# A planner's costs, from estimates to measured durations, and a margin behind the landing of raw weights

## The chip, the cores and the metric

The kernel runs on one core of a Trainium2 chip. Time is device microseconds (us) of one execution, lower is better. Five engines work side by side, each through its own list of instructions in order: TensorE (PE for its matmuls, PEld for its weight loads), VectorE (DVE), ScalarE (ACT), GpSimd (POOL) and SyncE (SP), which issues nearly all transfers.

## What is computed

Attention over 8 batches and 8 heads (576 positions, head size 64) with a window of 128 positions and a bias that falls with distance, and on its output (4608 tokens of 512 numbers) a gated feed-forward layer of width 1536. All inputs of the second part come as 64-bit floats.

```python
scores = scale * np.matmul(q, k.transpose(0, 1, 3, 2))
scores = np.where(mask, scores + bias[None], -1000000000.0)   # 0 <= rel < 128
scores = scores - np.max(scores, axis=-1, keepdims=True)
attn = np.exp(scores)
attn = attn / (np.sum(attn, axis=-1, keepdims=True) + 1e-09)
x = np.matmul(attn, v)             # transposed to (4608, 512)
gate = 1.0 / (1.0 + np.exp(-(x @ w_gate)))
val = x @ w_val
out = gate * val @ w_out
```

## The kernel before

**Attention.** A unit is one batch and one pair of heads; there are 32, of 9 blocks of 128 rows each, so 288 blocks. `scores` sends a run of eight blocks (four for the first units) through TensorE (line 440) into four PSUM banks, in a mode that splits the array into quarters of 64 rows by 64 columns. VectorE puts the window's far side in place (line 457) and adds the bias and takes the row maximum in one operation (line 465); ScalarE takes the exponential and the row sum (line 469). Three blocks make a triple, of which there are 96: `probabilities` divides them by their sums (a scaling for each block, on ScalarE, line 547, or on VectorE, line 548), TensorE transposes the three (line 554), a copy takes them out of PSUM and GpSimd cuts them into two masked halves (line 565). The values matmuls follow, for the first 11 units in `values` (line 592), for the others in `split_values` (line 511): two phases in the same quartered mode, usually one on either side of a scores run.

**First pass.** For the first 3072 tokens and the first 4 of 12 slices of the hidden width, gate and value products are made while attention still runs (line 640; 576 matmuls in all, in groups of three, called chunks here). Their weights are decoded from 64-bit words by `decode`: a transfer of 512 KB into one of two raw buffers (`wraw`), a scaling on ScalarE (line 331), a shift and two merges on VectorE (lines 332 and 335); then a high part and a remainder are formed (lines 195, 196, 204), since a product is made of three matmuls on split numbers.

**Second pass and output.** When attention has ended, its buffers are given back, the attention output is read again from device memory (`later_xr`), seven combinations of it are made (`xc`, lines 737, 195, 196, 204), and the other slices (and these four for the remaining tokens) follow as seven products in place of eight (line 774, 2016 matmuls, with the sums and gates of lines 781, 785 and 789). Their weights (`w2s`, seven slots) are decoded, combined and split on VectorE and ScalarE while these products run. The last stage does the same for the output weights (line 904, 1260 matmuls).

**What sets the order.** Nothing in the code orders the engines by hand. Every operation is put down with `g.add`: engine, cost in us, what it reads and writes, a wish (`want`), a `slack` that is added to the time at which its readers or it may go, and sometimes other engines that could do it. `Graph.order` then plays this list: again and again it takes the operation that can start and end soonest by these costs, chooses the engine, and notes a start; the program is written out in the order of the starts. First-pass and second-pass products have the lowest wish, so they go wherever the plan believes TensorE free. The costs decide the order only; what the chip takes is its own matter.

In `order`, an operation becomes ready like this, and `d.slack` is the place at which the change's new margin enters:

```python
same = o.eng == "PE" and d.eng == "PE"
d.ready = max(d.ready, o.start + (o.cost if same else o.lat + d.slack))
```

Of the kernel before, what the change touches and what calls it, by code (L numbers as in the profile page):

```python
# [20 lines left out]
DM, DFF = 512, 1536  # L21
# [34 lines left out]
SLACK = 0.1  # L56
W0, WSTEP = 20.0, 2.0
SWITCH = 0.36
WARM = 30.0
YIELD = {"DVE": 0.1, "POOL": 0.0}  # L60
NRAW = 2
# [3 lines left out]
def as32(ap):  # L65
    return ap.bitcast(F32)
# [102 lines left out]
def act_cost(n, psum=False):  # L169
    return (0.05 if psum else 0.1) + n * 0.00084  # L170
# [3 lines left out]
def attention_gated_ffn(ctx: ExitStack, tc: tile.TileContext, qd, kd, vd, wg, wv, wo, out):  # L174
    nc = tc.nc
    ctx.enter_context(tc.manual_schedule())
    g = Graph()
# [29 lines left out]
    mm = [ps_m.tile([P, NB], F32, name=f"mm{i}") for i in range(8)]  # L207
# [114 lines left out]
    def decode(src, fc, bits, kb, want, release=0.0):  # L322
        s = raws[0] % NRAW
        raws[0] += 1
        kr = ("wraw", s)
# [3 lines left out]
        raw = lambda: T(moe, f"wraw{s}", [P, DM, 2], I32)  # L329
        move(lambda: raw().rearrange("p f t -> p (f t)"), lambda: src[fc].bitcast(I32), [], [kr], want, 512, True, release)  # L330
        g.add("ACT", act_cost(DM), lambda: nc.scalar.mul(as32(bits()), as32(raw()[:, :, 1]), 2.0 ** -112), [kr], [kb], want)
        g.add("DVE", dve_cost(DM), lambda: nc.vector.tensor_scalar(
# [78 lines left out]
    def scores(blks, pend=None):  # L411
# [31 lines left out]
        for (u, i), (r, a) in zip(blks, spot):  # L443
            used.setdefault(bank_of(r, a), []).append((u, i, a % 2))
        cost = sum(max(0.216 if i == 0 else 0.33 for (u, i), (r, b) in zip(blks, spot) if b == a) for a in {a for r, a in spot})
        reads = [("qr", u.l, i) for u, i in blks] + [("kr", u.l, j) for u, i in blks for j in (i - 1, i) if j >= 0]
# [40 lines left out]
    def split_values(u, want, reads, writes, release):  # L487
# [15 lines left out]
        def phase(n, reads, writes, release):  # L503
# [3 lines left out]
            def matmuls():  # L507
                for e, r, h, j, a, b, first, last in runs:
# [4 lines left out]

            g.add("PE", 0.85, matmuls, need + [("vr", u.l)] + ([("turn", u.s)] if n else []) + reads, both + writes, want, slack=0.0 if n else SLACK,
                  release=release, mode=1)
# [20 lines left out]
    def probabilities(u, i0):  # L536
# [8 lines left out]
        for e in range(n):  # L545
            args = lambda e=e: (pb()[:, e], pb()[:, e], st()[:, 6 + e:7 + e])
            g.add("ACT", 0.3, lambda args=args: nc.scalar.mul(*args()), [(kst, 6)], [(kpb, e)], want,  # L547
                  ways=[("DVE", 0.16, True, lambda args=args: nc.vector.tensor_scalar_mul(*args()))])

        z = work()  # L550
# [4 lines left out]

        g.add("PE", 0.11 * n + 0.1, transpose, [(kpb, e) for e in range(n)], [("mm", z)], want, slack=slack)
        copy(lambda: both(), lambda: mm[z][:, 0:n * P].rearrange("p (a q) -> p a q", a=n), n * P, [("mm", z)], [kb], want, psum=True)
# [528 lines left out]
```

## Time and profile before

| | us |
|---|---|
| median of 3 runs | 981.16 |
| lowest and highest of them | 978.7 and 981.19 |
| the profiled execution's own time | 983.17 |
| its span, first to last instruction | 981.5 |
| TensorE busy, matmuls | 964.4 (98%) |
| TensorE busy, weight loads | 833.6 (85%) |
| VectorE busy | 771.6 (79%) |
| ScalarE busy | 531.7 (54%) |
| GpSimd busy | 126.5 (13%) |

The ends of matmuls in the profile are modelled and overlap, so 98% is no measure of how well TensorE is fed; it shows where TensorE stood idle, not how fast it went elsewhere. The shares are means over stages that differ: attention with the first pass until about 312 us, the second pass until about 709 us, the output stage until the end. Scores and values matmuls stand twice in the trace for each one in the program's listing.

### The profile page before, as it was taken

Reading aid. Unit: us, or ns where it says so; the run is one execution under the profiler, and the core shown is the slowest. Engines: PE = TensorE matmul, PEld = TensorE weight load, DVE = VectorE, ACT = ScalarE, POOL = GpSimd, SP = SyncE. Lnnn points to the kernel's source line nnn. Section 1 sums busy time; section 2 is a strip of 40 time slices with the busy share of each in tenths; the row PEclk is TensorE's granted clock in tenths of the full one; section 3 lists DMA queues with packets and bytes.
Section 4 is the critical chain, followed back from the end, with each engine's and each line's share of the span. In section 5 each row is a group of like instructions: output and inputs, shape, how many; then the busy total and the mean of one; then the engine's idle time right before and its main releaser. Section 6 shows DMA issues by size and latency. Waiting matters only on the chain.

```text
span 981.5 us, 18510 instructions
## 1 busy us (share of the span) xinstructions
PE 964.4 (98%) x6588; PEld 833.6 (85%) x6588; DVE 771.6 (79%) x1933; ACT 531.7 (54%) x1413; POOL 126.5 (13%) x213
## 2 busy tenths in 40 slices
PE   8899999999999999999999999999999999999998
PEld 7666788888878999999988888888878888889998
DVE  8998879977767999937984885793578977877783
ACT  8998878878874556434543443352344433333341
POOL 2333445333333000000000100000000000000000
PEclk9999999999999999999999999999999999999999
DMA  8868877775715535334374274469775435262601
GB/s 312 272 207 298 302 229 271 252 251 167 254 59 174 185 106 188 121 117 151 150 273 172 119 278 150 162 242 344 250 272 189 163 99 190 64 193 81 194 17 65
DMA packets 82078, 186.03 MB, mean 190 GB/s; under 512 B 7745, under 2 KB 36801, under 8 KB 81985
## 3 DMA queue, kind: packets, MB, share of 16 engines
q1 hardware_dynamic: 81840, 184.71, 54.7%
q8 instruction: 52, 0.85, 0.4%
q14 instruction: 42, 0.34, 0.1%
q10 hardware_dynamic: 144, 0.13, 0.0%
HBM read 122.95 MB, written 61.87 MB: 188 GB/s over the span
## 4 chain that ended last, share of the span: by engine, by line
PE 80%; DVE 8%; ACT 6%; DMA 4%; issue 1%; POOL 0%; POOLq 0%; ACTq 0%; DVEq 0%; SPq 0%
PE mm L774 40%; PE mm L904 25%; PE mm L640 7%; PE mm L440 3%; PE mm L511 2%; ACT pb L469 2%; PE mm L554 1%; DVE mm L457 1%; DVE first L204 1%; DVE pb L465 1%; DMA hid<-later_hs 1%; DVE wbits L335 1%; PE mm L592 1%; DMA rows_h<-hid 1%; DMA wraw<-in_moe_w_gate_dram 1%
## 5 line engine op out<-in xcount | busy, mean ns | idle before, releaser
L774 PE MATMUL mm<-xc,w2s 128*128 128x384 f32 (+1 forms) x2016 | 404.4, 362 | 0.2 <-DVE xc L204 0.2
L774 PEld LDWEIGHTS mm<-xc,w2s 128*128 128x128 f32 x2016 | 363.8, 188 | 40.7 <-DVE xc L204 0.6
L904 PE MATMUL mm<-duo,wo 128*128 128x512 f32 (+1 forms) x1260 | 259.2, 367 | 1.6 <-DVE duo L204 1.6
L904 PEld LDWEIGHTS mm<-duo,wo 128*128 128x128 f32 x1260 | 229.2, 188 | 31.6 <-DVE duo L204 2.0
L640 PE MATMUL mm<-first,first 128*128 128x512 f32 x576 | 155.6, 407 | 1.4 <-ACT sg L651 0.9
L640 PEld LDWEIGHTS mm<-first,first 128*128 128x128 f32 x576 | 101.6, 189 | 23.7 <-ACT sg L651 1.9
L785 ACT ACTIVATE sg<-mm 128x384 f32<-128x384 f32 (+1 forms) x96 | 52.2, 545 | 110.6 <-PE mm L774 71.5
L781 DVE TENSOR_TENSOR mm<-mm,low 128x384 f32<-128x384 f32 (+1 forms) x96 | 60.5, 630 | 64.1 <-PE mm L774 64.0
L195 ACT COPY low<-mm 128x384 f32<-128x384 f32 (+1 forms) x95 | 50.7, 535 | 73.6 <-PE mm L774 70.5
L469 ACT ACTIVATE pb<-pb,st 128x128 f32<-128x128 f32 x216 | 84.8, 401 | 1.6 <-DVE st L465 1.3
L565 POOL TENSOR_SCALAR_AFFINE_SELECT pt<-early_h 128x384 f32<-128x384 f32 x96 | 53.2, 572 | 108.0 <-ACT early_h L195 106.4
L565 POOL TENSOR_SCALAR_AFFINE_SELECT pt<-early_xr 128x384 f32<-128x384 f32 x96 | 52.1, 567 | 54.6 <-ACT early_xr L195 54.5
L457 DVE COPY_PREDICATED mm<-early_h,mm 128x256 f32<-128x256 int32 (+1 forms) x144 | 49.1, 392 | 6.3 <-PE mm L440 6.0
L465 DVE CUSTOM_DVE_ANT_0 pb<-mm,early_h 128x128 f32<-128x128 f32 x216 | 51.2, 282 | 0.0
L511 PEld LDWEIGHTS mm<-pt,vr 64*64 64x64 f32 x924 | 37.2, 132 | 10.5 <-issue 4.3
L547 ACT ACTIVATE pb<-pb,st 128x128 f32<-128x128 f32 x131 | 43.0, 398 | 0.1
L195 ACT COPY early_xr<-mm 128x384 f32<-128x384 f32 (+3 forms) x78 | 33.8, 446 | 16.5 <-PE mm L511 12.5
L469 ACT ACTIVATION_READ_ACCUMULATOR pb<-pb,st 128x1 f32 x216 | 42.7, 198 | 0.0
L542 DVE TENSOR_SCALAR st<-st 128x3 f32<-128x3 f32 x96 | 23.8, 249 | 23.8 <-ACT pb L469 12.4
L511 PE MATMUL mm<-pt,vr 64*64 64x192 f32 (+2 forms) x924 | 41.2, 285 | 0.8 <-ACT turn L520 0.8
L789 DVE SCALAR_TENSOR_TENSOR later_hs<-sg,later_hs 128x384 f32<-128x384 f32 (+1 forms) x48 | 29.9, 622 | 10.4 <-ACT sg L785 10.3
L781 DVE TENSOR_TENSOR later_hs<-mm,later_hs 128x384 f32<-128x384 f32 (+1 forms) x48 | 29.8, 621 | 10.5 <-ACT sg L785 6.8
(138 smaller groups left out, 1229.9 us busy)
## 6 DMA issues: line engine op xcount, KB each, us to landing
hid<-later_hs SPq DMA_DIRECT2D x24, 512.0 KB, 3.4
wo<-stash_o SPq DMA_DIRECT2D x12, 896.0 KB, 7.5
vr<-in_v_dram SPq DMA_DIRECT2D x32, 288.0 KB, 4.8
hid<-later_hs SPq DMA_DIRECT2D x24, 384.0 KB, 2.8
stash_o<-wtmp SPq DMA_DIRECT2D x12, 768.0 KB, 4.0
wraw<-in_moe_w_gate_dram SPq DMA_DIRECT2D x16, 512.0 KB, 5.1
wraw<-in_moe_w_val_dram SPq DMA_DIRECT2D x16, 512.0 KB, 4.5
kr<-in_k_dram SPq DMA_DIRECT2D x11, 576.0 KB, 4.4
```

The source lines that it names most:

```text
L195: g.add("ACT", act_cost(n, psum), lambda: nc.scalar.copy(out(), src()), reads, writes, want, release=release, ways=[("DVE", dve_cost(n, ps ...
L457: g.add("DVE", dve_cost((a1 - a0) * P, psum=True), lambda b=b, a0=a0, a1=a1: nc.vector.copy_predicated(quads(b)[:, a0:a1, 1:3], before[:, ...
L465: g.add("DVE", 0.21, lambda: nc.vector.tensor_tensor_reduce(pb()[:, e], sp[b][:, a, D:D + P], relm[u.p][:, w], op0=ALU.add, op1=ALU.min, s ...
L469: g.add("ACT", 0.39, lambda: nc.scalar.activation(pb()[:, e], pb()[:, e], AF.Exp, bias=st()[:, e:e + 1], scale=-1.0, accum_out=st()[:, 3 + ...
L511: nc.tensor.matmul(mm[WORK[h]][e * D:(e + 1) * D, a - e * S - cuts[h]:b - e * S - cuts[h]], vraw(u)[r * D:r * D + D, c], seen, start=first ...
L547: g.add("ACT", 0.3, lambda args=args: nc.scalar.mul(*args()), [(kst, 6)], [(kpb, e)], want, ways=[("DVE", 0.16, True, lambda args=args: nc ...
L565: nc.gpsimd.affine_select(pt(u)[:, f0:f0 + 2 * n - 1:2, :], both(), [[0, n], step], cmp, 0.0, base=0, channel_multiplier=mult)
L640: nc.tensor.matmul(mm[s][:, 0:wd], w.tile(kind, wi, i)[:, c * P:(c + 1) * P], xpart(x, c)[:, 0:wd], start=(k == 0 and c == 0), stop=(k == ...
L774: nc.tensor.matmul(mm[b][:, 0:N2], w.tile2(i, wp)[:, wk, c * P:(c + 1) * P], combo(k, xp, N2)[:, c], start=(start and c == 0 and j == 0), ...
L781: g.add("DVE", dve_cost(N2, psum=True), lambda: nc.vector.tensor_tensor(o(), bk(b)(), a(), op=ALU.add), [("mm", b), *reads] if okeys else ...
L785: g.add("ACT", act_cost(N2, psum=True), lambda: nc.scalar.activation(sg[h](), bk(b)(), AF.Tanh, scale=0.5), [("mm", b)], [("sg", h)], F)
L904: nc.tensor.matmul(mm[b][:, 0:N2], wo2(2 * q + m, wp)[:, k, j * P:(j + 1) * P], duo(xp)[:, m], start=(k in (0, 3, 1) and q == 0 and m == 0 ...
```

## The change

Six edits of the planner's figures. The scaling of raw weights may start, in the plan, only 4.0 us after the planned landing of its transfer (the margin enters through `slack`). A pair of blocks in a scores run costs 0.29 (0.19 where it is a first block) instead of 0.33 (0.216); one phase of the split values 0.71 instead of 0.85; a scaling of probabilities on VectorE 0.19 instead of 0.16; a triple of transposes 0.095 x 3 = 0.285 instead of 0.11 x 3 + 0.1 = 0.43. No instruction's operands, shapes or buffers are changed; the number of some instructions changes with the engine that the plan chooses for them, and the filler matmuls on `ident` (line 277) with its gaps.

```diff
+LATE = 4.0
@@ decode
-        g.add("ACT", act_cost(DM), lambda: nc.scalar.mul(as32(bits()), as32(raw()[:, :, 1]), 2.0 ** -112), [kr], [kb], want)
+        g.add("ACT", act_cost(DM), lambda: nc.scalar.mul(as32(bits()), as32(raw()[:, :, 1]), 2.0 ** -112), [kr], [kb], want, slack=LATE)
@@ scores
-        cost = sum(max(0.216 if i == 0 else 0.33 for (u, i), (r, b) in zip(blks, spot) if b == a) for a in {a for r, a in spot})
+        cost = sum(max(0.19 if i == 0 else 0.29 for (u, i), (r, b) in zip(blks, spot) if b == a) for a in {a for r, a in spot})
@@ split_values
-            g.add("PE", 0.85, matmuls, need + [("vr", u.l)] + ([("turn", u.s)] if n else []) + reads, both + writes, want, slack=0.0 if n else SLACK,
+            g.add("PE", 0.71, matmuls, need + [("vr", u.l)] + ([("turn", u.s)] if n else []) + reads, both + writes, want, slack=0.0 if n else SLACK,
@@ probabilities
-                  ways=[("DVE", 0.16, True, lambda args=args: nc.vector.tensor_scalar_mul(*args()))])
+                  ways=[("DVE", 0.19, True, lambda args=args: nc.vector.tensor_scalar_mul(*args()))])
-        g.add("PE", 0.11 * n + 0.1, transpose, [(kpb, e) for e in range(n)], [("mm", z)], want, slack=slack)
+        g.add("PE", 0.095 * n, transpose, [(kpb, e) for e in range(n)], [("mm", z)], want, slack=slack)
```

The changed kernel's lines stand one further down than those of before (331 is 332, 774 is 775, and so on), since a constant is added above them.

Nearly every row of the order moves. Three places show how. The first is SyncE's list where attention ends: `xs` is the attention output on its way to device memory, `later_xr` the same data read back for the second pass, `hid` a finished piece of the first pass, `wraw` raw weights. Before:

```order
L200 DMA xs_108<-early_xr 128x576
L200 DMA xs_108<-xt_536 128x576
L200 DMA hid_117<-early_hs_1094 128x512
L200 DMA later_xr<-xs_106 128x4x384
L200 DMA later_xr<-xs_107 128x4x384
L200 DMA hid_132<-early_hs_1217 128x512
L200 DMA wraw_213<-in_moe_w_gate_dram 128x1024
L200 DMA wraw_220<-in_moe_w_val_dram 128x1024
```

and now:

```order
L201 DMA xs_108<-early_xr 128x576
L201 DMA xs_108<-xt_506 128x576
L201 DMA later_xr<-xs_106 128x4x384
L201 DMA later_xr<-xs_107 128x4x384
L201 DMA hid_117<-early_hs_1008 128x512
L201 DMA hid_132<-early_hs_1117 128x512
L201 DMA later_xr<-xs_108 128x4x384
L201 DMA later_xr<-xs_107 128x4x192
L201 DMA later_xr<-xs_108 128x4x192
L201 DMA wraw_221<-in_moe_w_val_dram 128x1024
L201 DMA wraw_215<-in_moe_w_gate_dram 128x1024
```

The first two reads of `later_xr` now follow the last write of `xs` directly, and the raw weights stand behind all five reads. On TensorE, in the same place, the number of first-pass matmuls behind the last values matmul falls from 66 (22 chunks) to 27 (9 chunks), and the second pass opens with combination `xc0` where it opened with `xc3`.

The second is VectorE's list from its last copy of attention's output on (`early_hs` is the first pass's gating, `w2s` a slot of second-pass weights, `low` and `later_xr` as targets are combinations). Before:

```order
L196 COPY xt_536<-mm_78 128x256
L659 SCALAR_TENSOR_TENSOR early_hs_1094<-sg_975,mm_71 128x512
L196 CAST w2s_4228<-wbits_396 128x512
L196 CAST w2s_4228<-tt 128x1280
L659 SCALAR_TENSOR_TENSOR early_hs_1217<-sg_979,mm_72 128x512
L204 TENSOR_TENSOR w2s_4243<-wbits_396,w2s_4228 128x512
L204 TENSOR_TENSOR w2s_4243<-tt,w2s_4228 128x1280
L204 TENSOR_TENSOR w2s_4258<-wbits_390,w2s_4230 128x512
L332 TENSOR_SCALAR wbits_396<-wbits_396 128x512
L332 TENSOR_SCALAR tt<-tt 128x512
```

and now:

```order
L197 COPY xt_506<-mm_78 128x256
L660 SCALAR_TENSOR_TENSOR early_hs_1008<-sg_859,mm_71 128x512
L205 TENSOR_TENSOR w2s_4290<-wbits_438,w2s_4279 128x512
L205 TENSOR_TENSOR w2s_4297<-wbits_418,w2s_4287 128x512
L205 TENSOR_TENSOR w2s_4290<-tt,w2s_4279 128x1280
L660 SCALAR_TENSOR_TENSOR early_hs_1117<-sg_933,mm_72 128x512
L197 CAST xc_4305<-later_xr 128x2x384
L205 TENSOR_TENSOR xc_4305<-later_xr,xc_4305 128x2x384
L205 TENSOR_TENSOR xc_4307<-later_xr,xc_4307 128x2x384
L333 TENSOR_SCALAR wbits_438<-wbits_438 128x512
```

Before, the decoding of a further slot's weights (lines 332 and 335) stands ahead of the first combination; now two combinations come first.

The third is ScalarE's list early in attention, at the third scaling of raw weights. Before, it stands behind 54 exponentials:

```order
L195 COPY early_xr<-mm_78 128x288
L469 ACTIVATE early_h_147,st_366<-early_h_147,st_366 128x128 x2
L469 ACTIVATE early_xr,st_433<-early_xr,st_433 128x128
L195 COPY early_xr<-mm_77 128x288
L469 ACTIVATE early_xr,st_433<-early_xr,st_433 128x128 x2
L331 ACTIVATE wbits_390<-wraw_213 128x512
L195 COPY early_xr<-mm_78 128x384
```

and now behind 63:

```order
L196 COPY early_xr<-mm_78 128x384
L470 ACTIVATE pb_274,st_217<-pb_274,st_217 128x128 x2
L470 ACTIVATE pb_297,st_231<-pb_297,st_231 128x128 x3
L332 ACTIVATE wbits_418<-wraw_215 128x512
L196 COPY xt_506<-mm_77 128x288
L548 ACTIVATE pb_306<-pb_306,st_298 128x128
```

All later scalings of the early stage move back likewise.

## The prediction

> **What bounds the kernel now.** I read the page's busy times, then a table of windows cut at the kernel's stages (span, then busy microseconds and count for PE, PEld, DVE, ACT and POOL, granted clock, DMA share, GB/s), then the chain and the timeline where stages meet.
>
> ```profile
> PE 964.4 (98%) x6588; PEld 833.6 (85%) x6588; DVE 771.6 (79%) x1933; ACT 531.7 (54%) x1413; POOL 126.5 (13%) x213
> ...
> 0.00:42.00 42.00, 36.78 (x423) 28.68 (x424) 36.83 (x215) 36.73 (x150) 12.10 (x27) 0.96 0.84 299
> 42.00:112.00 70.00, 64.92 (x634) 48.10 (x633) 64.88 (x290) 66.45 (x252) 25.94 (x48) 1.00 0.75 257
> 112.00:297.50 185.50, 184.08 (x2194) 151.54 (x2192) 145.69 (x717) 147.06 (x575) 74.09 (x131) 1.00 0.65 217
> 316.00:404.00 88.00, 88.00 (x507) 87.45 (x506) 85.21 (x153) 48.21 (x90) 3.46 (x1) 1.00 0.47 150
> 404.00:709.00 305.00, 305.00 (x1462) 266.97 (x1461) 212.68 (x315) 125.19 (x213) 4.88 (x5) 1.00 0.53 196
> 730.00:981.50 251.50, 247.74 (x1210) 219.83 (x1210) 195.41 (x209) 90.06 (x113) 0.00 (x0) 1.00 0.39 126
> ```
>
> From 112 us on TensorE sets the time: it lacks 1.4 us in 185.5 and nothing from 316 to 709. Before that no engine is alone: from 42 to 112 us it stands idle for 5.1 of 70 us, while VectorE is 93% and ScalarE 95% busy. The number of matmuls is the same in both kernels, so a new order can only fill or open holes. There are two places for that: the stage before 112 us, and the seam at 312 us where attention hands over to the second pass. The turn to the output stage at 709 us is touched by no edit.
>
> The same table for the first pass's matmuls alone (line 640; PE, PEld, clock, DMA, GB/s) and for the transposes (line 554) tells how far the program is at those marks:
>
> ```profile
> 0.00:42.00 42.00, 0.38 (x2) 0.36 (x3) 0.96 0.84 299
> 42.00:112.00 70.00, 26.58 (x96) 16.43 (x94) 1.00 0.75 257
> ...
> 0.00:42.00 42.00, 6.26 (x33) 3.69 (x33) 0.96 0.84 299
> 42.00:112.00 70.00, 14.00 (x74) 8.69 (x75) 1.00 0.75 257
> ```
>
> By 112 us some 36 triples of transposes (107 of them) and 98 first-pass matmuls are out.
>
> **The costs that the planner now uses.** A stretch of the chain from the stage that TensorE fills (start, length, what), then VectorE's scalings in it earlier on:
>
> ```profile
> 263.16 0.85 PE mm L511 x19
> 264.00 1.31 PE mm L440 x27
> 265.32 0.76 PE mm L511 x18
> 266.08 0.89 PE mm L640 x3
> 266.97 0.66 PE mm L554 x6
> 267.63 0.69 PE mm L640 x3
> ...
> 275.15 3.43 PE mm L640 x15
> ...
> 18.54 0.96 DVE pb L548 x5
> ```
>
> A triple of transposes takes 0.66 / 2 = 0.33 us: the plan had 0.43 and gets 0.285. Values, scores, values take 2.92 with one change of array mode in them; the change costs 0.89 - 0.69 = 0.20, so 2.72 bare: the plan had 0.85 + 1.32 + 0.85 = 3.02 and gets 0.71 + 1.16 + 0.71 = 2.58. A scaling on VectorE takes 0.96 / 5 = 0.19, the new figure. So the plan was 0.10 to 0.30 too long on these and is now 0.05 to 0.15 too short: nearer. No instruction becomes shorter by it. What moves is the filler: three matmuls of the first pass (a chunk) take 0.69 to 0.70 us, and the planner puts one wherever it believes TensorE free. Counted over the listed orders: with the 36th triple 32 chunks are out before and 38 after; after the last values matmul 22 stand before and 9 after.
>
> **Edit by edit, early stage.** The six chunks, 6 x 0.70 = 4.2 us, go into the stage with 5.1 us of visible idleness. Their own load elsewhere is small, one gating on VectorE or one tanh on ScalarE per four chunks:
>
> ```profile
> L659 DVE SCALAR_TENSOR_TENSOR early_hs<-sg,mm 128x512 f32<-128x512 f32 x21 | 14.3, 681 | 4.7 <-PE mm L640 4.6
> ```
>
> So six chunks bring about one such operation of 0.7 us. I let them fill holes, -4.2; bounds 0 (every hole lies where a chunk's data isn't there) and -5.1. The later scaling of raw weights acts on ScalarE, which is in order: behind a waiting scaling stand exponentials and the copies out of PSUM, and VectorE's mask and TensorE's transposes wait for those. Line 331's rows up to 115 us (what ended the idle time before it: us, times) show what it waited:
>
> ```profile
> L331 ACT ACTIVATE wbits<-wraw x10: 650/672/707, 19.1 to 114.7; 128x512 f32<-128x512 f32 x10
>   DMA wraw<-in_moe_w_val_dram: 1.7, 1
>   DMA wraw<-in_moe_w_gate_dram: 0.9, 2
> ```
>
> That is 2.6 us. Besides, up to the 36th triple ScalarE's list holds two weight scalings (0.67 each) and three casts of much the same length fewer, about 3 us; VectorE's holds seven scalings of probabilities more (7 x 0.19) and about as much less of the decoding, so its sum stays. With VectorE at 93% I don't believe the whole 5.6: the stage ends between 0 and 4 us sooner, and I take 1.0, near VectorE's side, since that engine gets no lighter. The raw buffers are held up to 4 us longer, which I cost at nothing: the first chunk stands behind the 12th triple instead of the 11th, but at the 19th the new list is ahead, 10 chunks to 6.
>
> **Mode changes.** Counted, 103 become 112; five of the nine lie in the early stage beside idle time, four behind it: 4 x 0.20 = +0.8 (bounds 0 and 1.8).
>
> **The seam.** The timeline before (start, us, engine and line, [idle before]); SPq rows are transfers issued:
>
> ```profile
> 297.49 15.26 PE L640 MATMUL mm<-first,first 128*128 128x512 f32 x66
> 312.58 2.62 PE L774 MATMUL mm<-xc,w2s 128*128 128x384 f32 x14
> 315.44 1.84 PE L774 MATMUL mm<-xc,w2s 128*128 128x384 f32 x9 [0.25 <-DVE xc L204]
> ...
> 298.14 0.32 SPq L200 DMA_DIRECT2D xs<-xt  x1
> 299.89 0.32 SPq L200 DMA_DIRECT2D hid<-early_hs  x1
> 300.39 0.98 SPq L200 DMA_DIRECT2D later_xr<-xs  x2
> ...
> DMA to landing us min/median/max: 3.6/4.4/6.6
> ...
> 308.56 0.95 DVE L737 TENSOR_TENSOR low<-later_xr 128x768 f32<-128x768 f32 x1
> ...
> 358.36 0.56 DVE L196 CAST xc<-later_xr 128x768 fp32r<-128x768 f32 x1
> 359.02 0.96 DVE L204 TENSOR_TENSOR xc<-later_xr,xc 128x768 fp32r<-128x768 f32 x1
> ```
>
> Call V the moment at which the last values matmul ends (297.5). Before, 66 matmuls cover V to 312.6, and the rows `later_xr`, needed for the second pass, are asked for at V + 2.9, behind a write of `hid` that waits for VectorE. After, they stand on SP right behind `xs<-xt`: V + 0.65 + 0.35 = V + 1.0, the second one 0.4 later, and with the longest landing of these reads, 6.6, they are there at V + 8.0. The first combination is then cast (0.66 with its follow-up) and its low part taken (0.95): the first matmuls go at V + 8.7, the third waits until V + 9.6. The cover is now 9 x 0.70 = 6.3 us. So TensorE idles 2.4, then 0.5 for the low part, and some 0.7 while VectorE makes the seven combinations one by one: 3.6 against the 0.25 seen before, net +3.3. Bounds: with the median landing of 4.4 the first matmuls go at V + 6.5, so +1.1; with `hid` writes sharing the transfer engines I allow once more the 2.2 between median and longest, so +5.5.
> [...]
>
> **What is late next.** VectorE prepares the second pass's weights from V on, and must have made the seventh slot when the seventh slice of its first group of tokens starts, then seven new combinations:
>
> ```profile
> 345.05 1.49 DVE L204 TENSOR_TENSOR w2s<-tt,w2s 128x1280 fp32r<-128x1280 f32 x1
> 354.25 0.57 DVE L781 TENSOR_TENSOR mm<-mm,low 128x384 f32<-128x384 f32 x1 [0.57 <-PE mm L774]
> ```
>
> Before, that slot is ready at 346.5 and first used near 356 (six slices of 42 matmuls behind 312.6, at 88.00 / 507 = 0.174 us each; VectorE already waits for TensorE at 354): 10 us of slack. After, with 6 us less cover and the slot's last part ten operations (10 x 0.56) later in VectorE's list, about nothing is left; the new list of TensorE goes round it by starting the second group. I take 0; bounds 0 and +2.
>
> **Sum**, against the profiled span of 981.5 (that execution's time is 983.17; the median of the runs is 981.16, so I carry the difference over to the median): -4.2 - 1.0 + 0.8 + 3.3 + 0 = -1.1. Predicted 980.1 us. V itself moves from 297.5 to about 297.5 + 13 x 0.70 - 5.2 + 0.8 = 302.2.
>
> **The rivals.** (1) Faster: ScalarE alone was the early stage's limit. For it: 95% busy, and the waits of transposes for its copies, below; against it: VectorE's 93%. Then the stage ends 4 us sooner instead of 1.0, and with the median landing the seam costs 1.1: -4.2 - 4.0 + 0.8 + 1.1 = -6.3, 974.9; halfway there, 977.5. Chance 0.28.
> (2) Slower: the cover is gone and the holes stay. The moved chunks then stretch the stage before 112 us by what they take, because holes there come from exponentials and copies that a chunk in front delays too; only the seam's price is left: 0 + 0.8 + 3.3 to 5.5, so 985.3 to 987.5. It decides as soon as fewer than two of the six chunks find a hole. For it: the holes are small, the longest put down to one wait there 0.9 us. Against it: VectorE and ScalarE have 5% or more left. Chance 0.17. The wait both rivals speak of, from 42 to 115 us (us, times, longest):
>
> ```profile
> PE mm L554 <- ACT early_xr L195: 1.7, 2, 0.9
> PEld mm L554 <- ACT early_xr L195: 3.2, 4, 1.4
> ```
>
> (3) The plan's figures change the list but not the time, since TensorE is full from 112 us on and the two places cancel: 981.2, within 1. This runs into my own forecast; both together 0.47.
> (4) The clock. The rows between 34 and 40 us (last columns as above):
>
> ```profile
> 34.00:36.00 2.00, 1.32 (x18) 0.88 (x18) 2.00 (x15) 2.00 (x10) 1.51 (x4) 1.00 0.95 340
> 36.00:38.00 2.00, 2.00 (x20) 1.25 (x20) 2.00 (x14) 1.89 (x10) 0.44 (x1) 0.52 0.58 182
> 38.00:40.00 2.00, 2.00 (x23) 1.96 (x21) 1.73 (x11) 0.47 (x2) 0.00 (x0) 0.63 0.86 276
> ```
>
> After a sparse stretch the granted clock falls to about half for some 3.4 us. If the seam's hole of 2.4 to 3.6 us does the same, half of 3.4 us is lost: +1.7, so 981.8, and with the late landing 984.0. Chance 0.08. [...]
>
> **How the numbers follow.** A measurement of this kernel tells 0.3%, 2.9 us, from no change: its three runs lie 2.5 apart. My forecast and rival (3), 0.47, lie inside, with a tenth of it spilling to either side; (1) is faster; (2) and the late part of (4) are slower. That gives faster 0.31, same 0.45, slower 0.24. The likeliest case alone spans 977.5 to 983. The range reaches from (1)'s far end to near (2)'s: 974.5 to 985.5.
>
> **What would show it.** First-pass matmuls by the 36th triple: 114 by about 111 us, if the holes were filled; if that mark comes at 115 or later, (2) holds. V near 302, `later_xr` asked for about 1 us behind it, a hole of 2 to 4 us before the first matmul of line 775, and full TensorE from some 316 us on. TensorE idle before a slice in the 40 us after that would mean VectorE's weights are late, which I cost at nothing. The last two stages must take what they took, 305 and 251.5 us; if they differ by over 1 us, my sum is wrong whatever its total.

## The result, and the profile after

The changed kernel takes 987.71 us (median, 986.61 to 988.38) against 980.89 for the kernel before on the same chip: a ratio of 1.0073, 95% interval 1.0055 to 1.0091. It is slower; 980.1 was forecast, in a range that ended at 985.5. The profiled execution took 988.38 us, its span 986.7.

The page's busy line and its costliest group, then the same windows as before (span, busy us and count of PE, PEld, DVE, ACT, POOL, granted clock, DMA share, GB/s):

```profile
PE 965.4 (98%) x6604; PEld 838.4 (85%) x6604; DVE 771.7 (78%) x1936; ACT 533.4 (54%) x1405; POOL 123.7 (13%) x218
...
L775 PE MATMUL mm<-xc,w2s 128*128 128x384 f32 (+1 forms) x2016 | 408.7, 364 | 9.9 <-ACT later_hs L196 6.8
...
42.00:112.00 70.00, 67.86 (x661) 53.40 (x661) 64.94 (x285) 66.65 (x250) 25.39 (x48) 0.99 0.82 267
112.00:297.50 185.50, 185.23 (x2181) 153.68 (x2179) 149.31 (x724) 147.83 (x565) 68.44 (x126) 1.00 0.66 216
316.00:404.00 88.00, 87.18 (x502) 86.58 (x501) 83.65 (x148) 43.90 (x85) 4.10 (x4) 1.00 0.49 157
404.00:709.00 305.00, 298.01 (x1414) 259.82 (x1414) 208.23 (x308) 126.16 (x211) 13.69 (x12) 0.99 0.51 189
730.00:981.50 251.50, 251.50 (x1228) 223.01 (x1227) 199.90 (x212) 93.04 (x115) 0.00 (x0) 1.00 0.42 134
```

Attention is better fed than before: TensorE's idle time from 42 to 112 us falls from 5.1 to 2.1 us, from 112 to 297.5 from 1.4 to 0.3. The loss is in a stage that had none: between 404 and 709 us TensorE lacks 7.0 us, 6.8 of them in one wait on `later_hs`. Where that lies is seen when the starts of the same matmul are set side by side (us; counted in the traces; the experiments' columns are read further down):

| mark | before | after | x1 | x2 | x3 | x4 | x5 | x6 | x9 |
|---|---|---|---|---|---|---|---|---|---|
| 36th triple of transposes | 112.0 | -1.5 | -0.7 | +1.3 | -2.4 | +3.4 | -0.8 | -5.5 | -0.6 |
| last values matmul | 297.3 | +1.9 | +2.7 | +4.7 | -2.7 | +9.3 | +2.6 | -8.0 | +2.7 |
| 1st matmul of the second pass | 312.6 | -5.1 | -4.2 | -2.2 | -2.7 | +2.8 | -4.3 | +0.9 | -4.2 |
| 300th | 365.3 | -2.5 | -2.9 | -0.9 | -2.7 | +4.9 | -3.0 | +0.6 | -2.8 |
| 1800th | 667.7 | -2.0 | -1.8 | -0.8 | -2.7 | +5.4 | -3.1 | +2.1 | -2.3 |
| 1900th | 690.4 | +7.3 | -1.8 | +0.7 | -1.7 | +6.3 | -3.1 | +2.1 | -2.3 |
| 1st of the output stage | 717.1 | +7.1 | -1.8 | +0.6 | -1.9 | +6.2 | -3.2 | +2.8 | -0.5 |
| last | 977.6 | +5.2 | -1.1 | -1.4 | -3.8 | +4.3 | +6.8 | +0.9 | -2.4 |

The changed kernel enters the second pass 5.1 us ahead and is still 2.0 ahead at its 1800th matmul. A hundred matmuls later it is 7.3 behind. The output stage gives 1.9 back: before, it has a hole of 1.6 us at 728 us, and now none. (The profiled execution of before lies 2 us above the median of its runs, so a column reads about 2 us too well against medians.)

**The place.** The windows of the changed kernel around it, same columns:

```profile
665.00:670.00 5.00, 5.00 (x23) 4.11 (x23) 0.00 (x0) 0.59 (x1) 0.00 (x0) 1.00 1.03 425
670.00:675.00 5.00, 5.00 (x24) 4.14 (x23) 2.61 (x5) 2.30 (x4) 0.00 (x0) 1.00 0.85 348
675.00:680.00 5.00, 2.03 (x9) 1.33 (x8) 4.90 (x11) 0.41 (x1) 0.00 (x0) 1.00 0.16 52
680.00:685.00 5.00, 1.16 (x3) 0.97 (x4) 2.23 (x2) 0.64 (x2) 0.00 (x0) 0.66 0.77 315
685.00:690.00 5.00, 5.00 (x17) 3.92 (x16) 1.74 (x3) 2.11 (x4) 0.00 (x0) 0.66 0.08 9
```

First the transfers are full and VectorE has nothing to do, then VectorE alone works, then TensorE resumes at half clock. The timeline names the chain (start, us, engine and line, [idle before <- what ended it]; SPq rows are issues of transfers), and the row behind it is the landing time of the two `wraw` transfers:

```profile
648.43 1.91 SPq L201 DMA_DIRECT2D rows_xr<-hid  x4
654.06 2.33 SPq L201 DMA_DIRECT2D wraw<-in_moe_w_out_dram  x2
672.91 0.66 ACT L332 ACTIVATE wbits<-wraw 128x512 f32<-128x512 f32 x1
679.77 2.11 SPq L201 DMA_DIRECT2D stash_o<-wtmp  x2
683.20 0.59 ACT L196 COPY later_hs<-mm 128x512 f32<-128x512 f32 x1 [7.01 <-DMA stash_o<-wtmp]
683.84 6.53 PE L775 MATMUL mm<-xc,w2s 128*128 128x512 f32 x18 [6.81 <-ACT later_hs L196]
...
DMA to landing us min/median/max: 13.7/14.1/14.4
```

And the same steps in the kernel before, with their landing:

```profile
633.18 0.42 SPq L200 DMA_DIRECT2D wraw<-in_moe_w_out_dram  x1
643.57 0.42 SPq L200 DMA_DIRECT2D wraw<-in_moe_w_out_dram  x1
646.52 0.67 ACT L331 ACTIVATE wbits<-wraw 128x512 f32<-128x512 f32 x1
648.34 1.91 SPq L200 DMA_DIRECT2D rows_xr<-hid  x4
657.05 3.00 SPq L200 DMA_DIRECT2D stash_o<-wtmp  x2
...
DMA to landing us min/median/max: 4.0/4.1/4.2
```

These are output weights, prepared during the second pass: `prepare_o` has six pairs to decode, split and write to device memory (`stash_o`). It is called with a `release`, a time on the planner's own clock ahead of which a pair's transfers may not go. Neither the diff nor the prediction has these lines, and they decide:

```python
OUT0, OSTEP = 470.0, 36.0
...
for n in range(NFC // 2):          # n = 0 .. 5: the last pair is released at 470 + 5 x 36 = 650
    prepare_o(n, 2.0e6 + n, OUT0 + OSTEP * n)
```

The clock reading stands; the program under it moved. The plan now believes most of attention's operations shorter, so at its 650 it is further on in the program. On the chip the last pair's transfers go out at 654 and 656 us instead of 633 and 644, now behind nine transfers of the 6 us ahead of them on the same queue (four `rows_xr` reads of the output stage, two writes of `wtmp` for the pair before, two reads of `w2s`, one write of `hid`); at 403 to 425 GB/s they land after 14 us instead of 4. The first scaling follows 26 us later than before, the writes of `wtmp` 22 to 23. `wtmp` shares its memory with two of four buffers for hidden values (`later_hs`) that only the second pass's last group of tokens uses: `ffn2` takes four there (`ends`), elsewhere two. The copy into one of them waits for the write, TensorE for the copy, and the clock is halved for 6.8 us from 681.6 on, of which 4.6 lie behind the hole (it ends at 683.8) and cost, by an estimate from the halved clock, half of that, 2.3. With the 6.8 us of idleness that makes 9.1 of the 9.3 us that the table shows between the 1800th matmul and the 1900th.

**The seam** went about as forecast. Timeline of the changed kernel where attention ends:

```profile
299.37 6.42 PE L641 MATMUL mm<-first,first 128*128 128x512 f32 x27
301.06 0.92 SPq L201 DMA_DIRECT2D later_xr<-xs  x2
306.85 0.83 ACT L196 CAST xc<-later_xr 128x768 fp32r<-128x768 f32 x1 [2.36 <-DMA later_xr<-xs]
307.52 0.62 PE L775 MATMUL mm<-xc,w2s 128*128 128x384 f32 x2 [1.74 <-DVE xc L197]
308.51 4.78 PE L775 MATMUL mm<-xc,w2s 128*128 128x384 f32 x17 [0.38 <-DVE xc L205]
```

V is 299.4. `later_xr` is asked for at V + 1.7, the second pass begins at V + 8.1, the idle time is 1.74 + 0.38 = 2.1 us. The first combination needs the first of the two reads only, which landed at V + 7.3 (306.77); the second landed at V + 9.3.

### The profile page after: what moved, and what is told of

The parts are those of the page before. It is cut to its first block, busy times and chain, and to the rows that moved or that the text cites. A ratio compares the mean times of both kernels' runs of the same rounds, so it can differ in the third digit from the quotient of the medians.

```text
span 986.7 us, 18540 instructions
## 1 busy us (share of the span) xinstructions
PE 965.4 (98%) x6604; PEld 838.4 (85%) x6604; DVE 771.7 (78%) x1936; ACT 533.4 (54%) x1405; POOL 123.7 (13%) x218
## 4 chain that ended last, share of the span: by engine, by line
PE 93%; DVE 3%; ACT 2%; issue 1%; DMA 1%; POOL 0%; SPq 0%; DVEq 0%; POOLq 0%; ACTq 0%
PE mm L775 39%; PE mm L905 26%; PE mm L641 13%; PE mm L441 5%; PE mm L555 3%; PE mm L512 3%; PE mm L593 2%; PE mm L278 1%; ACT pb L470 1%; DMA later_xr<-xs 1%; DVE w2s L205 0%; DMA stash_o<-wtmp 0%; DVE mm L782 0%; POOL pt L566 0%; DVE tt L205 0%
## 5 line engine op out<-in xcount | busy, mean ns | idle before, releaser
L775 PE MATMUL mm<-xc,w2s 128*128 128x384 f32 (+1 forms) x2016 | 408.7, 364 | 9.9 <-ACT later_hs L196 6.8
L641 PEld LDWEIGHTS mm<-first,first 128*128 128x128 f32 x576 | 101.6, 188 | 22.8 <-DVE first L197 2.2
L196 ACT COPY low<-mm 128x512 f32<-128x512 f32 (+1 forms) x94 | 50.2, 536 | 78.7 <-PE mm L775 63.2
L470 ACT ACTIVATE pb<-pb,st 128x128 f32<-128x128 f32 x216 | 84.7, 400 | 1.0 <-DVE st L466 0.9
L566 POOL TENSOR_SCALAR_AFFINE_SELECT pt<-early_xr 128x384 f32<-128x384 f32 x96 | 50.1, 547 | 58.8 <-ACT early_xr L196 55.9
L548 ACT ACTIVATE pb<-pb,st 128x128 f32<-128x128 f32 x119 | 40.3, 404 | 1.7 <-DVE turn L521 1.0
L196 ACT COPY later_hs<-mm 128x384 f32<-128x384 f32 (+1 forms) x46 | 24.6, 534 | 30.0 <-PE mm L775 16.8
```

The source lines that it names most:

```text
L196: g.add("ACT", act_cost(n, psum), lambda: nc.scalar.copy(out(), src()), reads, writes, want, release=release, ways=[("DVE", dve_cost(n, ps ...
L470: g.add("ACT", 0.39, lambda: nc.scalar.activation(pb()[:, e], pb()[:, e], AF.Exp, bias=st()[:, e:e + 1], scale=-1.0, accum_out=st()[:, 3 + ...
L566: nc.gpsimd.affine_select(pt(u)[:, f0:f0 + 2 * n - 1:2, :], both(), [[0, n], step], cmp, 0.0, base=0, channel_multiplier=mult)
L641: nc.tensor.matmul(mm[s][:, 0:wd], w.tile(kind, wi, i)[:, c * P:(c + 1) * P], xpart(x, c)[:, 0:wd], start=(k == 0 and c == 0), stop=(k == ...
L775: nc.tensor.matmul(mm[b][:, 0:N2], w.tile2(i, wp)[:, wk, c * P:(c + 1) * P], combo(k, xp, N2)[:, c], start=(start and c == 0 and j == 0), ...
```

## The experiments

All twelve change one or two places of a kernel shown. Medians are given with the ratio to the kernel before measured beside it (median 981.2 to 981.6), and its interval. Holes that the expectations give as 0.84, 1.76, 1.9 and 3.6 us measure 0.68, 1.60, 1.72 and 3.42 in the timelines.

**Two rivals for the stall.** Either the fixed release alone made it, or the margin on the scaling of output weights. Three kernels tell them apart.

x1 against the changed kernel, then x2 against the changed kernel, then x3 against the kernel before:

```diff
@@ x1
-OUT0, OSTEP = 470.0, 36.0
+OUT0, OSTEP = 446.0, 36.0
@@ x2
-        g.add("ACT", act_cost(DM), lambda: nc.scalar.mul(as32(bits()), as32(raw()[:, :, 1]), 2.0 ** -112), [kr], [kb], want, slack=LATE)
+        g.add("ACT", act_cost(DM), lambda: nc.scalar.mul(as32(bits()), as32(raw()[:, :, 1]), 2.0 ** -112), [kr], [kb], want, slack=LATE if src is not wo else 0.0)
@@ x3
-OUT0, OSTEP = 470.0, 36.0
+OUT0, OSTEP = 482.0, 36.0
```

> The changed kernel with one number undone in effect: the six preparations of output weights are released 24 us earlier on the planner's clock (446 instead of 470 for the first). Theory R (the release times are absolute on the planner's clock, which the new costs set back against the chip by 11 to 20 us, so the sixth preparation's loads fall behind a row of large transfers and its stores hold the buffers that the last group's hidden values need): loads of the last pair near 630 us, no stall of TensorE near 677 us, no half clock there, 976 to 978.5 us. Theory M (the new margin of 4 us behind landings makes the preparations late by itself): the margin is still there, a stall of 3 us or more stays, 981 to 985 us.

Measured: 982.25 us, ratio 1.0015 [0.9995, 1.0034].

> The changed kernel without the margin of 4 us for output weights alone; all releases as in it. Theory M: the stall near 677 us goes, 976 to 978.5 us. Theory R: the loads are issued as late as in the changed kernel (behind 41 writes of hidden values, near 654 us), the scalings at most 4 us sooner; the stall shrinks from 7.0 to between 2 and 5 us and the clock may stay whole: 980 to 985 us.

Measured: 981.53 us, 1.0008 [0.9993, 1.0024].

> The kernel before with one number changed: the output weights' preparations are released 12 us later on the planner's clock (482 instead of 470), with no margin and all old costs. Theory R: the last pair of loads falls behind the same row of transfers, a stall of 3 to 8 us of TensorE appears near 680 us, with the clock at half behind it: 985 to 991 us. Theory M: nothing happens, 980 to 982 us.

Measured: 980.41 us, 0.9995 [0.9980, 1.0009].

The rows of the writes that the hidden buffers wait for (median ns, first and last start) and, for x2 and x3, TensorE's holes there. x1:

```profile
L201 SPq DMA_DIRECT2D stash_o<-wtmp x2: 320/320/320, 655.4 to 658.0; - x2
```

x2:

```profile
L201 SPq DMA_DIRECT2D stash_o<-wtmp x2: 320/320/320, 673.7 to 675.5; - x2
...
677.56 1.66 PE L775 MATMUL mm<-xc,w2s 128*128 128x512 f32 x6 [0.68 <-ACT low L196]
679.43 10.95 PE L775 MATMUL mm<-xc,w2s 128*128 128x512 f32 x47 [0.20 <-ACT later_hs L196]
```

x3:

```profile
L200 SPq DMA_DIRECT2D stash_o<-wtmp x2: 319/319/319, 669.8 to 672.0; - x2
...
675.62 14.58 PE L774 MATMUL mm<-xc,w2s 128*128 128x512 f32 x63 [0.68 <-ACT low L195]
```

Neither rival holds alone. Of the 22.8 us by which the first write of `wtmp` is later than before (657.0 to 679.8), 16.7 stay without the margin (673.7) and cost nearly nothing: they use up slack. The last 6.1 come with the margin, and they are the stall. The margin does this in two ways: its order puts more transfers ahead of the last pair's, so that the first lands at 668.5 instead of 665.2 in x2, and the scaling then starts 4.4 us behind this landing instead of 0.8. A late release with the old costs (x3) has one hole of 0.7 us there, and x2 and x4 have one of the same size; all three end with a copy into `low`, not into a hidden buffer, and what made them is not shown. The times were missed even where the place was right. With the stall gone, 976 to 978.5 us was expected of x1 (by R) and x2 (by M): x1 gets back the hole at 727 us that the changed kernel had lost (1.7 us), and x2 is 2.8 us later than the changed kernel when attention ends. x3 was to stall for 3 to 8 us by R and didn't.

What counts is how late the writes are against TensorE. The second write's issue minus the start of the 1800th matmul of the second pass, and TensorE's idle time there, over the kernels of this study (x5, read below, leaves this memory alone):

| | x1, x7, before | x6, x10, x11 | x8 | x9 | x12 | x3, x4 | x2 | after |
|---|---|---|---|---|---|---|---|---|
| second write behind the 1800th, us | -8.0 | -5.8 | -3.8 | -2.5 | +2.3 | +7.0 | +8.5 | +15.8 |
| idle, put down to these writes | 0 | 0 | 0 | 0 | 0 | 0 | 0.2 | 6.8 |

Up to about 8 us nothing waits; beyond, the stall grows about one for one, as far as two kernels can tell (x2 and after: 7.3 us later, 6.6 us more).

**Is it the shared memory?** x5 lets the last group use two hidden buffers like all others, so that it never asks for `wtmp`'s memory.

```diff
-            e = turns[0] % (4 if ends else 2)
+            e = turns[0] % 2
```

> The changed kernel, whose last group uses two buffers for hidden values in place of four, so that it doesn't take over the memory of the output weights' temporary (wtmp). Theory (the 7 us stall runs over that memory: late landing, late scaling, late store of wtmp, copy of the hidden values, TensorE): the stores of the last pair stay as late as in the changed kernel, 679 to 682 us, but TensorE has no hole of over 1.5 us near 677 and no half clock behind it; time 978.5 to 982.5. Rival (the stall comes of the transfers themselves, so that the second pass's weights would be late with any buffers): the hole near 677 stays at 5 us or more and the time at 986 to 988.5. If two buffers are too few for the last group, small holes of under 1 us are spread over 690 to 720 us.

Measured: 989.26 us, 1.0083 [1.0061, 1.0104]. By the time alone, the rival won; by the place, the theory. The writes, then the timeline near 677 us and where the output stage starts (`rows_hs` is a read for the output stage, `csum` a sum that its second product needs):

```profile
L201 SPq DMA_DIRECT2D stash_o<-wtmp x4: 320/357/419, 649.4 to 682.4; - x4
...
667.63 22.60 PE L775 MATMUL mm<-xc,w2s 128*128 128x512 f32 x99
...
713.87 8.32 PE L905 MATMUL mm<-duo,wo 128*128 128x512 f32 x36
717.73 0.36 SPq L201 DMA_DIRECT2D rows_hs<-hid  x1
726.68 1.22 DVE L860 TENSOR_TENSOR csum<-rows_xr,rows_hs 128x1024 f32<-128x1024 f32 x1
729.03 1.22 PE L905 MATMUL mm<-duo,wo 128*128 128x512 f32 x2 [6.84 <-ACT duo L196]
731.49 3.78 PE L905 MATMUL mm<-duo,wo 128*128 128x512 f32 x8 [1.23 <-DVE duo L205]
```

The writes are as late as ever, 682.4, and the hole at 677 is gone: the 1900th matmul comes 3.1 us ahead of before's. So the stall does run over that memory. But the output stage then starts 10.3 us ahead of the changed kernel's and finds its rows not read yet: 6.8 us of idleness at 722, 1.2 more behind it, and the clock at half for 10.2 us from 727.2 on. The table's column shows it: -3.2 at the first output matmul, +6.8 at the last. This second hole is the edit's own doing: the two `rows_hs` reads take over the memory of just the two hidden buffers that now serve to the end. In x5 they go at 717.7 and 724.3, each directly behind the landing of a write of `hid`, 3.9 and 10.4 us after the output stage's first matmul; in the kernel before they go at 697.3 and 707.6, in the changed one at 709.9 and 716.9, ahead of it. Slow transfers alone don't explain it: in the changed kernel these reads take longer to land (8.2 and 9.4 us; 7.9 and 5.3 in x5), and there is no hole.

**Half the shift.** x9 is x1 with 458.

```diff
-OUT0, OSTEP = 470.0, 36.0
+OUT0, OSTEP = 458.0, 36.0
```

> The changed kernel with the output weights released 12 earlier on the plan's clock, half of what x1 had. Theory (the stall is what the late release leaves of the slack, so it shortens one for one with the release): the last pair's stores move from 680-682 to 666-671 us, the 7.0 us are used up, no hole over 1 us near 677; and the hole at 727 us, which the changed kernel lost with its late stores, stays below 1 us if it hangs on them; 980 to 983. Rival (the stores come late for the traffic in 655 to 670 us and not for the release): they move by less than 6 us, a hole of 1 to 5 us stays, 983 to 987.

Measured: 981.46 us, 0.9992 [0.9976, 1.0008]. Its stores and its two raw transfers:

```profile
L201 SPq DMA_DIRECT2D stash_o<-wtmp x2: 319/320/320, 661.1 to 662.9; - x2
...
L201 SPq DMA_DIRECT2D wraw<-in_moe_w_out_dram x2: 425/606/786, 641.8 to 642.3; - x2
DMA to landing us min/median/max: 4.4/4.8/5.2
```

The stall is gone, but the size was misjudged: 12 us of release moved the stores by 18.7, not by 9 to 16. The transfers leave 12 to 14 us earlier and, ahead of the `rows_xr` reads, take 9.3 us less to land. Both causes named in the expectation act at once: the release, and the transfers that stand ahead. The hole at 727 us is gone as well, but another of 1.6 us came at 713.

**The margin and the costs, each alone.** x4 sets `LATE` to 0 in the changed kernel; x6 gives the kernel before a margin of 4 and leaves its costs.

```diff
@@ x4
-LATE = 4.0
+LATE = 0.0
@@ x6
-        g.add("ACT", act_cost(DM), lambda: nc.scalar.mul(as32(bits()), as32(raw()[:, :, 1]), 2.0 ** -112), [kr], [kb], want)
+        g.add("ACT", act_cost(DM), lambda: nc.scalar.mul(as32(bits()), as32(raw()[:, :, 1]), 2.0 ** -112), [kr], [kb], want, slack=4.0)
```

> The changed kernel with the margin set to 0 everywhere, new costs kept. Only 2 chunks of the first pass are left behind the last values matmul instead of 9. Theory R: the stall near 677 us stays at 2 to 5 us; the hole at the seam grows from 2.1 by 7 chunks of 0.70 us to about 7 us, with a half clock behind it; 982 to 988 us. Theory M: no stall near 677 us; with the larger hole at the seam 978 to 983 us.

Measured: 988.12 us, 1.0079 [1.0054, 1.0105].

> The kernel before with the margin of 4 on the raw weights' scaling alone, all costs as before; the order has 35 first-pass chunks behind the last values, where before has 22 and the changed kernel 9. Theory (the margin does harm only together with the new costs, which shift the plan's clock against the fixed releases): the last pair of output weights is stored by 664 us, no hole over 1 us near 677, none at the seam; 979.0 to 982.5. Rival (the margin is what costs, with any costs): stores at 670 or later with a hole of 3 us or more, 984 to 988.

Measured: 983.89 us, 1.0023 [1.0012, 1.0033]. TensorE's rows at the seam of x4:

```profile
306.74 1.66 PE L641 MATMUL mm<-first,first 128*128 128x512 f32 x6
315.42 1.01 PE L775 MATMUL mm<-xc,w2s 128*128 128x384 f32 x2 [7.02 <-ACT xc L196]
```

and in attention in x6:

```profile
155.87 1.09 PE L554 MATMUL mm<-ident,pb 128*128 128x128 f32 x5
160.38 0.47 PE L554 MATMUL mm<-ident,pb 128*128 128x128 f32 x1 [3.42 <-ACT pb L547]
```

The new costs alone lose as much as the whole change, and elsewhere: only 2 chunks are left behind the last values, the seam's hole is 7 us, and the clock is at half for 10.2 us from 310.4 on, 5.2 of them behind the hole. Theory R had this right and the stall wrong (2 to 5 us expected): the writes of `wtmp` come at 677.8 and 680.1, up to 2 us ahead of the changed kernel's, but the whole program is 5 us behind by then, and no hidden buffer waits for them. The last pair's transfers go out at 659.4 and 659.8, without any margin, and with the margin alone (x6) at 635.3 and 635.8: the new costs are what moves them. So in this change the margin pulled cover back to the seam, and the 7 us turned up at 677 instead. The margin alone costs 0.2%. Its theory had the writes (663.0 and 664.0) and the two places without a hole right, the time 1.4 us too low. Attention ends 8.0 us sooner only because 35 chunks are left for afterwards, where before leaves 22; the second pass starts 0.9 us later. There is no hole at the seam, but one order of ScalarE's work leaves TensorE idle for 3.4 us at 157, with 6.8 us of half clock (the profile's mean clock is 0.997), and two smaller holes (1.2 and 0.6 us) follow in the second pass.

**Other sizes, and a search for a version that beats both.** x7 and x8 are x1 and x9 with VectorE's scaling back at 0.16, which leaves 15 chunks behind the last values; x10 and x11 the kernel before with a margin of 2 and 8; x12 the kernel before with 476 for 470.

```diff
@@ x7 (x8 with 458.0), against the changed kernel
-OUT0, OSTEP = 470.0, 36.0
+OUT0, OSTEP = 446.0, 36.0
-                  ways=[("DVE", 0.19, True, lambda args=args: nc.vector.tensor_scalar_mul(*args()))])
+                  ways=[("DVE", 0.16, True, lambda args=args: nc.vector.tensor_scalar_mul(*args()))])
@@ x10 (x11 with slack=8.0), against the kernel before
-        g.add("ACT", act_cost(DM), lambda: nc.scalar.mul(as32(bits()), as32(raw()[:, :, 1]), 2.0 ** -112), [kr], [kb], want)
+        g.add("ACT", act_cost(DM), lambda: nc.scalar.mul(as32(bits()), as32(raw()[:, :, 1]), 2.0 ** -112), [kr], [kb], want, slack=2.0)
@@ x12, against the kernel before
-OUT0, OSTEP = 470.0, 36.0
+OUT0, OSTEP = 476.0, 36.0
```

> The changed kernel with the old cost of VectorE's scaling (0.16) and the output weights released 24 earlier on the plan's clock; 15 chunks stand behind the last values in place of 9. If the seam's hole (1.52 + 0.53 us) is the cover that ran out, it shrinks to under 0.7 us and the time is 1 to 2 us below the changed costs with the earlier release (982.25): 979.5 to 982. If the seam waits for something else, the hole stays at 2 us and the time at 982 to 983.

Measured: 983.47 us, 1.0030 [1.0010, 1.0049].

> As the run beside it, but released 12 earlier in place of 24. The slack of the last group is then between the two: no stall near 677 over 1 us if the stores stand by 672 us, and the hole of 1.9 us at 727 us, which came where the stores were done by 660 us and not where they were later, should be gone or below 0.5 us; 978 to 981. If that hole does not hang on the output weights, it stays at 1.9 us and the time at 980 to 982.

Measured: 982.54 us, 1.0026 [1.0010, 1.0042].

> The kernel before with a margin of 2 in place of none on the raw weights' scaling and nothing else; 25 first-pass chunks behind the last values. With a margin of 4 (x6) the last values' product ended 8.0 us before that of the kernel before, and a hole of 3.6 us at 157 us with the half clock behind it spent it. If that hole is an accident of one order of ScalarE's work, a margin of 2 is free of it and gains: last values 3 us or more ahead, 975 to 980. If a margin on the scaling always puts some of ScalarE's work in the way of the transposes, it is 981 to 985.

Measured: 982.02 us, 1.0009 [0.9990, 1.0028].

> As the run beside it with a margin of 8, 19 chunks behind the last values, 102 changes of mode. If what the margin does is a matter of its size, this is worse than 4 (983.9): 984 to 990. If it is an accident of each order, it may fall on either side: 976 to 985, with no relation to 2 and 4.

Measured: 986.33 us, 1.0043 [1.0031, 1.0056].

> The kernel before with the output weights released 6 later. Released 12 later (x3) it lost its hole of 1.76 us at 728 us and got one of 0.84 us at 675 us. If both hang on when the last pair's weights are stored, half the shift should leave neither, or less than 0.5 us of each: 978.5 to 980.5. If they are accidents of the order, a hole of 0.8 to 1.8 us stays at one of the two places: 980 to 982.

Measured: 982.71 us, 1.0010 [0.9993, 1.0028].

The seam of x7:

```profile
299.41 0.99 SPq L201 DMA_DIRECT2D later_xr<-xs  x2
308.57 1.57 ACT L196 CAST xc<-later_xr 128x768 fp32r<-128x768 f32 x2 [3.42 <-PE mm L641]
309.45 0.62 PE L775 MATMUL mm<-xc,w2s 128*128 128x384 f32 x2 [0.69 <-ACT xc L196]
311.61 1.65 PE L775 MATMUL mm<-xc,w2s 128*128 128x384 f32 x4 [1.54 <-DVE xc L205]
```

Fifteen chunks of cover leave a hole of 2.2 us, as nine did. There the first combination waits until a first-pass matmul ends, not for its transfer, so cover is worth nothing beyond the point at which another wait comes last; and smaller holes follow from 375 to 395 us. x8 has the same hole at the seam; its writes of `wtmp` have gone out by 667.4 us and the hole at 727 us is gone, as its expectation had it, but one of 0.9 us comes at 719 and the time is over both ranges. x10 is neutral, without the gain hoped for; x11 is the worst of the margins and loses at the seam, at 362 us (late weights) and at 447 us (late combinations); x12 keeps a hole of 1.0 us at 728 us, so the idea that half the shift removes both holes is wrong; its time too is above both ranges. No kernel beats the kernel before by more than the measurement can tell: x9 (0.9992) and x3 (0.9995) equal it.

## Why the prediction was wrong

The first pass's matmuls alone (PE, PEld, clock, DMA, GB/s) in the window up to 112 us, after:

```profile
42.00:112.00 70.00, 33.33 (x120) 20.99 (x120) 0.99 0.82 267
```

- **Early holes filled** (-4.2 - 1.0): right. The 36th triple comes at 110.5 us (about 111 forecast), with 114 first-pass matmuls ahead of it, as forecast, and by 112 us 120 are out, where 96 were (the forecast's 98 counts two that lie across the windows' common edge twice); the stage ended sooner though it did more.
- **Mode changes and the full stage** (+0.8): too high. V is 299.4, not 302.2, 2.8 less. 0.5 of it is the 36th triple, 1.1 the idleness from 112 to 297.5 us that fell from 1.4 to 0.3 and that I had left as it was; of the other 1.2 up to 0.8 can be the charge for mode changes. No run isolates these.
- **The seam** (+3.3, bounds 1.1 to 5.5): right in kind, mis-sized. 2.1 us of idleness against 0.25 makes +1.9: the second part of the hole measured 0.4 instead of 0.5, the wait between the seven combinations that I had put at 0.7, with no row behind it, didn't show, and the first matmul came at V + 8.1 instead of V + 8.7. That is two errors against each other: the reads were asked for 0.7 us later than forecast, but I made the first combination wait for the later read, and it needs the earlier one, which landed after 5.7 us and not 6.6.
- **VectorE's weights late** (0, bounds 0 to 2): 0.8 us of idleness at 356 us, ended by VectorE's low part of a slot of weights. The bounds held, the value taken did not.
- **Rival (4), the clock**: it happened in the profiled execution (from the 1st to the 100th matmul 1.5 us more than before and 1.3 more than x1; 1.7 forecast), and not in x1, with the same hole. See below.
- **The step that failed**: "The turn to the output stage at 709 us is touched by no edit", and its twin, "The last two stages must take what they took, 305 and 251.5 us". From 404 to 709 us TensorE was busy for 298.0 of 305 us and the stall's half clock came on top. I followed the changed order up to the seventh slot and stopped where the edited costs stop. But a release on the planner's clock couples every later stage to every cost ahead of it: shorter costs push what is released at a fixed reading to a later place in the program. The margin too acts wherever `decode` is called, on output weights too. And the slack of this path was never read off: by the table over the writes it was about 16 us against TensorE (-8.0 before, 8 allowed), and the change used 24. What the runs showed in that step's place: a fixed release and the margin together put the last writes of `wtmp` 22 to 23 us later, and a buffer that takes over their memory kept TensorE waiting for 6.8 us.

Up to the 1800th matmul the changed kernel was 2.0 us ahead, my sum said 1.1. That nearness is partly luck: the second pass began 3.4 us earlier than my terms give (307.5, not V + 8.7 = 310.9), and the half clock (1.5) and the late weights (0.8), both at nothing in the sum, took 2.3 of it back. With the stall removed in three ways (x1, x2, x9) the change measures 1.0015, 1.0008 and 0.9992, no change, which is the case that I gave the largest chance; the stall itself was in no case of mine. Rival (2) had the right sign, and its 985.3 to 987.5 came near the size, for a wrong reason: the early holes were filled.

## What to carry to other kernels

Where a planner orders the work, list every time that is given as a number on its clock and ask where it falls after the costs have changed; a cost that is nearer to the truth moves all of them. Read the slack of every path that ends in a buffer taken over by somebody else, not only the waits that the profile shows: before, this path had no wait at all. And a repair at one seam is judged at the next ones: here 7 us disappeared at 308 us (x4) and came back at 677 us.

## What the runs showed of the hardware

The stretches at half clock were whole steps of 3.41 us. In the profile of the changed kernel, up to its last matmul, they start at 39.90, 309.55 and 681.61 us, 79.0 and 109.0 steps apart, and last 3.41, 3.41 and 6.83 us; in that of before one starts at 36.06 us and lasts 3.41; at the holes of x4 and x5 the clock was at half for 10.2 us, three steps. What went with it, as far as these profiles show, was how busy TensorE was in the step ahead. The steps at the seam of the changed kernel:

```profile
306.14:309.55 3.41, 1.66 (x8) 1.34 (x9) 3.38 (x6) 2.18 (x4) 0.00 (x0) 1.00 0.84 320
309.55:312.97 3.42, 3.42 (x13) 3.42 (x12) 3.42 (x5) 2.52 (x5) 0.00 (x0) 0.50 0.00 1
```

and of x1, whose hole has the same size and, counted in such steps from x1's own stretch at half clock at 102.8 us (60.0 to 307.65), lies across a step's edge:

```profile
304.24:307.65 3.41, 2.36 (x11) 1.63 (x9) 3.41 (x5) 1.87 (x3) 0.00 (x0) 1.00 1.03 364
307.65:311.07 3.42, 2.36 (x12) 2.04 (x13) 3.39 (x6) 2.18 (x5) 0.00 (x0) 1.00 0.45 170
311.07:314.48 3.41, 3.41 (x22) 3.41 (x21) 3.41 (x6) 2.01 (x4) 0.00 (x0) 1.00 0.00 0
```

The step that was 49% busy was followed by half clock, the two that were 69% busy were not. In the profile of before the step ahead of its stretch was 63% busy, in the changed kernel's those ahead of its three 52, 49 and 0%. Over the fourteen profiles, apart from a kernel's first step and those from its last matmul on, all 19 steps at 52% or less were followed by half clock; from 53 to 77% it went either way; above that it followed only where the clock was at half already. (In the step in which the last matmul ends, 34% and less was followed by half clock, and 45%, in x5, was not.) So the hole of 2 us at the seam cost 1.3 us more or not (the changed kernel against x1), by where it fell. One program's executions differ in their clock: the 31 of the kernel before that were measured beside x9 had means from 0.994 to 1.000, where one step at half takes off 0.0017 (half of 3.41 us in 981); where their steps lay is not on record.

The time to landing went with what was queued ahead: the same 512 KB landed 4.1 us after their issue in the kernel before, and 14.1 us after it in the changed one, behind nine other transfers and with the transfer engines full (DMA share 1.01 to 1.03 from 655 to 670 us) at 403 to 425 GB/s. In x9 they left 4 us ahead of the `rows_xr` reads and landed after 4.8.
